# First two batches of a sliding-window attention: bias and mask added by TensorE, 13 output buffers, a new written-out order

## The chip, the cores and the metric

The kernel runs on one core of one Trainium2 chip. The metric is the device time of one execution in microseconds (us); lower is better.

## The reference

```python
# q, k, v: (8 batches, 8 heads, 576 rows, 64)
scores = q @ k.T / 8                                   # per batch and head
rel = pos[:, None] - pos[None, :]
scores = where((rel >= 0) & (rel < 128), scores - slope[h] * abs(rel), -1e9)
x = concat_heads(softmax(scores) @ v)                  # (8, 576, 512); slope[h] = 2 ** -(h + 1)
W = (x @ w_q) @ (x @ w_k).T / 8                        # (576, 576) per batch
out = relu(W @ x) @ w_out                              # (8, 576, 512), float32
```

## The kernel before

Everything is written as named steps. A step has an engine, the steps that it depends on, and, on TensorE, a place in PSUM. PSUM is four pairs (0 to 3) of two banks of 512 float columns. The text ORDER lists all steps in program order as `name:engine`, with P for TensorE (and its pair and bank), A for ScalarE (ACT), D for VectorE (DVE), G for GpSimd (POOL), S for SyncE (SP). Each engine takes its steps strictly in that order; semaphores follow from the dependencies and from the reuse of buffers. So the sequence of the work is fixed by hand, and no scheduler moves anything.

A name is a kind, a batch and a part. The key blocks of a batch are 0 to 3 of 128 rows and 4 of 64; the heads of a unit are u = 0 (heads 0 to 3) or 1 (heads 4 to 7).

- **LF, Lq, Lk, Lt, Lv**: loads. LF are the six float loads of the first blocks, by SP and ACT. The others are issued by POOL (lines 378, 385, 391) and cast to float16; Lt holds the last 64 rows of q and k of two batches, in two DMAs. There are 109 POOL loads. Lw and Lwo (lines 442, 450) fetch the weights on SP's queue.
- **TF, TJ, TQ, TT** and their evictions **EF, EJ, ETQ, ETT**: transposes of q and k on TensorE through an identity matrix (line 251), and copies out of PSUM (lines 255 on ACT, 257 on DVE).
- **QK b.g.u** (line 571): scores of key block g against up to 256 query rows, for four heads, in one pair; 64-row weights, two heads side by side. **EXP** (line 591, ACT) takes the exponential of the whole pair, 1024 columns, into a float16 tile pt. **MUL** (line 598, DVE) multiplies pt by the tile bias (biasl for the last block), which holds exp(-slope * rel) inside the window and 0 outside.
- **PV b.q** (line 622): the product with v, with a column of ones for the sums. **RC** (line 652) and **X** (line 638), both on DVE, divide by the sums and write x. **XT, XTT** with **EXT, EXTT** transpose x.
- Two batches form a group. **WK, WT, WQ, G, MX, RM** work out relu(W @ x) without forming W: projections, the product G of projected keys and x, its product MX with the projected queries, and the eviction RM with the relu. EWK, EWT, EWQ and EG are the evictions between. CWQ and CW cast the weights.
- **OUT** (line 858), **EO** (eviction to a float buffer osb, line 868) and **DO** (store, lines 875 and 878, SP's queue) give the output. The osb buffers are a ring: each tile takes the place of the one allocated OSB tiles before it, and waits until that one has been stored. Float loads and weights use the same ring.
- **GT** makes the next store wait for a QK step, so that stores stay behind loads.
- **WM.i**: products of a zero tile with itself, 256 columns each (line 303), in stretches where TensorE would stand idle; WARM lists how many each stretch has. Their results are not used.
- Set-up steps on DVE: warm, wmc, ones, zeros, biasl, pads, idh (identity in float16); on POOL iota, ident, mask; on ACT bias. The mask tile wm holds rel inside the window and 1e9 outside.

In batches 0 and 1 each QK unit is followed by its own EXP and MUL, as in all others:

```python
s = add("QK", b, f"{g}.{u}", w, pe(0.225), need, em, banks=2, mode=1)
x = add("EXP", b, f"{g}.{u}", w + 0.6, {"ACT": (0.92, 1.02)}, [s, *oldp], ex, frees=[s])
mul[b, g, u] = add("MUL", b, f"{g}.{u}", w + 1.6, DVE(0.68),
                   [x, mkb if g < 3 else mkbl], ml)
```

Of the kernel before, what the change touches and what calls it, by code (L numbers as in the profile page):

```python
# [12 lines left out]
ALU = mybir.AluOpType  # L13
# [20 lines left out]
OSB = 15  # L34
# [11 lines left out]
WARM = (13, 2, 5, 7, 5, 10, 2, 4, 4, 2, 1, 1, 2, 3, 4, 5, 1, 1, 2, 10, 1, 2, 2)  # L46

ORDER = """
warm:D LF0.0.1.1:A LF0.1.0.0:S iota:G WM.0:P01 ident:G wmc:D LF0.0.0.1:S LF0.0.1.0:A ones:D
mask:G LF0.0.0.0:S LF0.1.0.1:S Lq0.2:G bias:A Lk0.1:G zeros:D TF0.1.0:P00 Lt0:G WM.1:P10  # L50
TF0.0.1:P01 EF0.1.0:A biasl:D TF0.0.0:P10 TF0.1.1:P00 WM.2:P20 Lk0.3:G EF0.0.0:A QK0.0.0:P1
EF0.1.1:D Lq0.3:G WM.3:P20 EF0.0.1:D EXP0.0.0:A idh:D Lk0.2:G QK0.0.1:P0 TJ0.2.0:P20 EXP0.0.1:A
TJ0.1.1:P21 EJ0.2.0:D Lk1.3:G WM.4:P30 EJ0.1.1:D MUL0.0.0:D QK0.1.1:P0 Lq1.3:G QK0.1.0:P1
EXP0.1.1:A WM.5:P30 Lq1.2:G EXP0.1.0:A MUL0.1.1:D TT0:P00 Lk1.2:G WM.6:P30 ETT0:D ETT1:A
TJ0.3.1:P01 Lk1.1:G MUL0.1.0:D WM.7:P30 EJ0.3.1:A MUL0.0.1:D TJ0.3.0:P00 Lq1.1:G WM.8:P30
EJ0.3.0:A TJ0.2.1:P01 Lk1.0:G QK0.3.0:P1 EJ0.2.1:D WM.9:P30 EXP0.3.0:A QK0.2.1:P0 Lq1.0:G
WM.10:P30 QK0.3.1:P2 WM.11:P30 EXP0.2.1:A TQ1.3:P10 Lk2.3:G WM.12:P11 ETQ1.3:D EXP0.3.1:A
QK0.2.0:P3 WM.13:P11 Lv0.0:G MUL0.2.1:D TQ1.2:P00 EXP0.2.0:A Lv0.1:G QK1.3.0:P1 ETQ1.2:D
WM.14:P20 EXP1.3.0:A MUL0.3.1:D Lv0.2:G QK1.2.0:P0 TQ1.1:P30 MUL0.2.0:D EXP1.2.0:A Lk2.2:G
QK1.2.1:P1 ETQ1.1:D WM.15:P20 EXP1.2.1:A Lv0.3:G MUL1.2.0:D QK1.1.1:P0 TQ1.0:P30 MUL1.3.0:D  # L60
EXP1.1.1:A Lq2.2:G QK1.1.0:P1 ETQ1.0:D WM.16:P31 QK1.3.1:P2 EXP1.1.0:A WM.17:P31 Lq2.3:G
MUL0.3.0:D PV0.0:P0 QK1.0.0:P3 MUL1.1.1:D EXP1.3.1:A Lv1.0:G MUL1.2.1:D QK1.0.1:P1 EXP1.0.0:A
Lv1.1:G MUL1.1.0:D PV0.1:P2 RC0.0:D EXP1.0.1:A Lv1.2:G X0.0:D PV0.2:P3 RC0.1:D Lk2.0:G X0.1:D
PV0.3:P0 WM.18:P11 RC0.2:D X0.2:D Lv1.3:G TQ2.2:P10 XT0.0:P11 MUL1.3.1:D ETQ2.2:A Lq2.0:G
TQ2.3:P20 MUL1.0.1:D WM.19:P21 ETQ2.3:A Lq2.1:G MUL1.0.0:D RC0.3:D EXT0.0:A PV1.1:P3 X0.3:D
Lk2.1:G QK2.2.0:P2 pads:D PV1.2:P0 RC1.1:D Lv0.4:G EXP2.2.0:A X1.1:D XT0.1:P10 Lv1.4:G wz:D
RC1.2:D QK2.2.1:P3 Lw:S EXT0.1:A X1.2:D PV1.0:P2 Lk3.1:G WM.20:P11 Lwo.2:S RC1.0:D PV1.3:P0
EXP2.2.1:A X1.0:D Lwo.0:S Lq3.1:G WM.21:P11 Lwo.1:S RC1.3:D XT1.0:P10 Lwo.3:S X1.3:D Lt1:G
TQ2.0:P11 EXT1.0:A XT1.1:P00 ETQ2.0:D WM.22:P20 TQ2.1:P01 EXT1.1:D Lq3.0:G PV0.4:P1 ETQ2.1:D
PV1.4:P2 RC0.4:D Lk3.0:G X0.4:D QK2.1.1:P0 QK2.0.0:P3 EXP2.1.1:A Lk3.2:G RC1.4:D QK2.0.1:P1  # L70
X1.4:D Lq3.2:G CWQ:A MUL2.2.1:D QK2.1.0:P0 EXP2.0.0:A XTT0:P20 WK0:P21 Lq4.1:G EXTT0:D
MUL2.1.1:D EXP2.0.1:A Lk3.3:G WT0:P20 EWK0:D WQ0:P30 EWT0:A MUL2.0.0:D Lv2.1:G EXP2.1.0:A G0:P31
EWQ0:D CW.2:A CW.0:D TQ3.1:P10 EG0:A Lq3.3:G CW.1:A ETQ3.1:D MX0.0:P0 MX0.2:P2 RM1.0:A TT2:P11
RM0.2:D RM0.0:A MX0.3:P3 Lt2:G RM1.2:D RM1.3:A MX0.1:P0 ETT2:D RM0.3:A TQ3.0:P10 CW.3:D RM1.1:A
RM0.1:D QK2.3.1:P2 Lv2.0:G OUT1.1:P30 EXP2.3.1:A ETQ3.0:D Lv3.0:G TQ3.2:P31 EO1.1:A MUL2.3.1:D
QK3.0.1:P0 QK2.3.0:P2 Lv2.2:G ETQ3.2:D DO1.1:S EXP3.0.1:A OUT0.3:P10 ETT3:D Lq4.0:G MUL2.0.1:D
EXP2.3.0:A QK3.0.0:P3 QK3.1.1:P0 MUL2.1.0:D Lk4.0:G GT3.0:S OUT1.3:P11 EO0.3:A MUL2.3.0:D
EXP3.1.1:A Lv2.3:G TQ3.3:P20 MUL2.2.0:D OUT1.0:P21 EXP3.0.0:A ETQ3.3:D Lv3.1:G OUT0.1:P10
MUL3.0.1:D EO1.0:A MUL3.0.0:D EO1.3:A QK3.1.0:P0 QK3.3.0:P3 Lk4.1:G MUL3.1.1:D EXP3.1.0:A
QK3.3.1:P2 GT3.1:S GT3.3:S OUT0.2:P11 EO0.1:D Lv3.4:G EXP3.3.0:A MUL3.1.0:D PV2.1:P0 Lv3.2:G  # L80
OUT1.2:P10 EXP3.3.1:A RC2.1:D MUL3.3.0:D Lv3.3:G PV2.2:P3 X2.1:D EO1.2:A QK3.2.1:P2 EO0.2:A
Lv2.4:G RC2.2:D PV2.0:P0 DO1.2:S X2.2:D EXP3.2.1:A OUT0.0:P10 DO0.3:S Lk4.2:G RC2.0:D X2.0:D
TT4:P11 EO0.0:A Lk4.3:G MUL3.3.1:D MX0.4:P3 QK3.2.0:P2 ETT5:A RMT0:D PV3.1:P0 Lq4.3:G GT3.2:S
EXP3.2.0:A XT2.0:P10 MUL3.2.1:D PV2.3:P3 Lq4.2:G RC3.1:D EXT2.0:A MUL3.2.0:D TQ4.0:P20
OUT1.4:P21 RC2.3:D Lq5.3:G X3.1:D ETT4:A ETQ4.0:A X2.3:D PV3.0:P1 TQ4.1:P00 RC3.0:D PV3.2:P3
EO1.4:A X3.0:D Lq5.1:G ETQ4.1:A XT2.1:P01 RC3.2:D X3.2:D XT3.0:P10 Lq5.2:G PV3.3:P2 EXT2.1:A
EXT3.0:D PV3.4:P3 Lq5.0:G RC3.3:D QK4.0.0:P1 X3.3:D PV2.4:P0 Lk5.1:G EXP4.0.0:A GT4.0:S DO1.0:S
RC3.4:D XT3.1:P20 DO1.3:S RC2.4:D Lk5.2:G X2.4:D TQ4.3:P21 EXT3.1:A QK4.0.1:P1 X3.4:D Lk5.3:G
TQ4.2:P00 EXP4.0.1:A WK2:P01 ETQ4.2:D Lk5.0:G ETQ4.3:A XTT2:P20 QK4.1.1:P1 Lk6.3:G EXTT2:D
WQ2:P30 EXP4.1.1:A EWK2:D Lv4.1:G MUL4.0.0:D WT2:P31 EWQ2:D QK4.2.1:P2 EWT2:A QK4.1.0:P0  # L90
EXP4.2.1:A MUL4.1.1:D G2:P10 Lv4.2:G GT4.1:S MUL4.0.1:D EXP4.1.0:A Lk6.2:G QK4.2.0:P3 EG2:D
TQ5.1:P11 EXP4.2.0:A GT4.2:S DO1.4:S Lv4.0:G MX2.0:P0 ETQ5.1:D MX2.2:P2 DO0.1:S RM2.0:A MX2.1:P3
RM3.2:D Lk6.0:G RM3.0:A TQ5.2:P10 RM2.2:D TQ5.3:P11 RM2.1:A Lv4.3:G MUL4.1.0:D RM3.1:A MX2.3:P0
QK4.3.1:P2 RM3.3:A Lq6.0:G ETQ5.3:D TQ5.0:P30 EXP4.3.1:A OUT3.0:P31 ETQ5.2:D Lv5.2:G MUL4.2.0:D
RM2.3:A QK5.3.0:P1 QK5.2.0:P2 ETQ5.0:D EXP5.3.0:A GT5.3:S OUT2.3:P00 GT5.2:S EO3.0:D Lk6.1:G
EXP5.2.0:A OUT3.1:P01 MUL4.3.1:D DO3.0:S MUL4.2.1:D Lv5.1:G EO2.3:A QK5.0.1:P1 QK4.3.0:P3
MUL5.3.0:D EXP5.0.1:A QK5.0.0:P2 Lv4.4:G GT4.3:S OUT2.0:P00 EO3.1:D GT5.0:S EXP4.3.0:A
MUL5.0.1:D Lq6.2:G PV4.2:P1 OUT3.3:P01 EXP5.0.0:A RC4.2:D Lq6.1:G X4.2:D PV4.0:P3 EO2.0:A
MUL4.3.0:D QK5.1.0:P1 QK5.1.1:P2 EO3.3:A RC4.0:D GT5.1:S OUT2.1:P00 Lv5.0:G X4.0:D EXP5.1.1:A
DO3.3:S MUL5.2.0:D TQ6.0:P01 Lq6.3:G EXP5.1.0:A MUL5.1.1:D PV4.1:P3 OUT2.2:P20 Lv5.3:G RC4.1:D  # L100
ETQ6.0:A X4.1:D PV4.3:P1 Lv5.4:G MUL5.1.0:D EO2.2:A QK5.2.1:P3 RC4.3:D Lq7.1:G QK5.3.1:P2
EXP5.2.1:A X4.3:D OUT3.2:P01 MUL5.0.0:D Lk7.0:G EXP5.3.1:A PV4.4:P1 MUL5.2.1:D TQ6.2:P30 Lk7.1:G
RC4.4:D EO3.2:A MUL5.3.1:D XT4.1:P31 ETQ6.2:A PV5.2:P2 X4.4:D Lq7.0:G TQ6.1:P01 EO2.1:A EXT4.1:D
Lt3:G MX2.4:P1 XT4.0:P30 RMT2:A DO2.1:S RC5.2:D TQ6.3:P00 X5.2:D DO2.2:S ETQ6.1:A PV5.1:P1
DO3.2:S ETQ6.3:D DO2.0:S PV5.0:P2 EXT4.0:A Lv6.1:G OUT3.4:P31 RC5.1:D RC5.0:D X5.1:D Lk7.2:G
X5.0:D QK6.0.1:P0 EO3.4:A PV5.3:P1 EXP6.0.1:A Lq7.2:G XT5.0:P20 RC5.3:D X5.3:D PV5.4:P3 EXT5.0:A
Lv6.0:G QK6.1.1:P0 RC5.4:D QK6.2.0:P1 X5.4:D EXP6.1.1:A XT5.1:P21 Lq7.3:G TQ7.1:P20 EXT5.1:D
EXP6.2.0:A Lk7.3:G QK6.2.1:P3 QK6.0.0:P0 MUL6.0.1:D WK4:P21 GT6.0:S EXP6.0.0:A ETQ7.1:D Lv6.3:G
XTT4:P10 MUL6.2.0:D TQ7.0:P11 EXP6.2.1:A QK6.1.0:P0 ETQ7.0:D WQ4:P20 EWK4:A GT6.1:S EXTT4:D
EXP6.1.0:A MUL6.1.1:D WT4:P21 Lv6.2:G MUL6.2.1:D EWQ4:A QK7.0.1:P3 TT6:P10 MUL6.1.0:D EWT4:A  # L110
Lv7.1:G QK7.0.0:P0 EXP7.0.1:A G4:P11 MUL6.0.0:D GT7.0:S DO3.4:S Lv7.0:G ETT6:D EXP7.0.0:A
DO3.1:S QK6.3.1:P2 DO0.2:S EG4:D Lv7.4:G TQ7.2:P30 GT6.2:S EXP6.3.1:A DO0.0:S ETT7:D Lv7.2:G
MX4.2:P0 ETQ7.2:D MX4.3:P1 RM4.2:A MX4.0:P2 RM4.3:D Lv7.3:G RM5.3:A PV6.1:P3 RM5.0:D RM4.0:A
MX4.1:P1 RM5.2:A MUL7.0.0:D Lv6.4:G TQ7.3:P20 RM4.1:A RC6.1:D QK6.3.0:P0 ETQ7.3:D RM5.1:A
OUT4.1:P21 EXP6.3.0:A X6.1:D QK7.2.1:P1 EO4.1:D QK7.3.1:P3 EXP7.2.1:A QK7.2.0:P0 MUL6.3.1:D
OUT5.0:P20 DO4.1:S GT7.2:S GT6.3:S DO2.3:S MUL6.3.0:D EXP7.2.0:A PV6.2:P1 MUL7.0.1:D OUT4.0:P21
EXP7.3.1:A RC6.2:D X6.2:D QK7.1.1:P0 EO5.0:A QK7.3.0:P3 MUL7.3.1:D QK7.1.0:P1 EXP7.1.1:A
OUT5.1:P20 MUL7.2.0:D EXP7.1.0:A MUL7.2.1:D OUT4.2:P00 MUL7.1.1:D EXP7.3.0:A PV6.3:P1 MUL7.1.0:D
OUT4.3:P01 RC6.3:D EO4.0:A X6.3:D EO5.1:A PV7.1:P3 DO4.0:S MUL7.3.0:D EO4.2:A DO5.0:S PV6.0:P1
PV7.2:P2 GT7.1:S EO4.3:A RC6.0:D DO4.2:S RC7.1:D X6.0:D XT6.1:P00 DO5.1:S OUT5.3:P01 DO4.3:S  # L120
RC7.2:D EXT6.1:A X7.1:D GT7.3:S X7.2:D PV7.0:P1 EO5.3:A PV7.3:P3 RC7.0:D XT6.0:P00 X7.0:D
DO5.3:S PV6.4:P2 EXT6.0:A RC7.3:D X7.3:D XT7.0:P01 PV7.4:P1 RC6.4:D EXT7.0:A X6.4:D XT7.1:P30
# [48 lines left out]
def kernel(  # L171
# [54 lines left out]
    def two(bank):  # L226
        return pairs[bank[0]]
# [725 lines left out]
```

## Time and profile before

| | |
|---|---|
| time of three runs | 142.67 us median (142.62 to 142.86) |
| the profiled execution | 142.51 us, its span on the core 140.4 us |
| busy, share of the span | TensorE 93%, ACT 84%, DVE 83%, POOL 68% |
| largest groups | EXP 64 x 1045 ns (ACT), MUL 48 + 16 x about 0.68 us (DVE) |
| DMA | 25.60 MB at a mean of 182 GB/s |

Busy times are those of the profiler; on TensorE products overlap, so a step's cost is read from one start to the next. "PEld" is the loading of weights, beside the products. A row of the timeline gives the start, the length of the merged group, engine, line, operation, output and input, and the count; brackets hold the idle time before it and what ended that.

### The profile page before, as it was taken

The numbers are of one execution on the slowest core, as the hardware profiler recorded it, in microseconds if no ns is written. First come the engines' busy times: TensorE is split into PE (matmuls) and PEld (weight loads), VectorE is DVE, ScalarE is ACT, GpSimd is POOL, SyncE is SP. The second block draws the span as 40 slices with busy tenths as digits, with TensorE's granted clock in tenths as the row PEclk, the third lists the DMA queues.
The fourth block names the chain that finished last, engine by engine and source line by source line (L and its number), as shares of the span: only waits on it lengthen the run. The fifth ranks groups of instructions, "written<-read, shape, count | busy, mean of one in ns | idle before, by whom it ended". The sixth has DMA issues, their size and how long they took to land.

```text
span 140.4 us, 4614 instructions
## 1 busy us (share of the span) xinstructions
PE 131.1 (93%) x1909; PEld 87.7 (62%) x1909; DVE 117.0 (83%) x270; ACT 117.8 (84%) x168; POOL 95.6 (68%) x118
## 2 busy tenths in 40 slices
PE   6999998999898999999999999999899999999970
PEld 5867655868664556788646566978446568753430
DVE  5866399998998999998899999989979999759330
ACT  4868899697599999998899999999989997748340
POOL 7999999999939998999969688996297000000000
PEclk9999999999999999999999999999999999999997
DMA  4999999999999999999999999999999979205593
GB/s 101 199 151 155 150 151 155 150 152 165 258 225 158 159 195 155 185 212 157 237 161 183 212 197 191 161 216 259 163 170 247 211 169 374 79 0 149 161 389 130
DMA packets 119477, 25.60 MB, mean 182 GB/s; under 512 B 114208, under 2 KB 114464, under 8 KB 119456
## 3 DMA queue, kind: packets, MB, share of 16 engines
q0 software_dynamic: 109264, 13.77, 154.7%
q1 hardware_dynamic: 9136, 11.28, 24.2%
q10 hardware_dynamic: 1056, 0.26, 0.8%
q8 instruction: 15, 0.25, 0.6%
q14 instruction: 6, 0.05, 0.1%
HBM read 29.62 MB, written 9.44 MB: 278 GB/s over the span
## 4 chain that ended last, share of the span: by engine, by line
PE 60%; ACT 15%; DMA 7%; DVE 6%; issue 5%; POOL 3%; ACTq 0%
PE pair L248 49%; PE pair L251 11%; ACT pt L591 10%; DMA natt<-in_k_dram 7%; POOL nat L378 2%; ACT rm L785 2%; DVE qkT L257 2%; DVE pt L598 1%; DVE x L638 1%; DVE osb L257 1%; ACT wout_sb L255 1%; ACT xT L255 1%; DVE inv L652 1%; POOL natt L385 1%; ACT wkt L255 0%
## 5 line engine op out<-in xcount | busy, mean ns | idle before, releaser
L591 ACT ACTIVATE pt<-pair 128x1024 f16<-128x1024 f32 x64 | 62.4, 1045 | 5.1 <-PE pair L248 5.0
L391 POOL DMA_DIRECT2D vt<-in_v_dram x40 | 34.7, 896 | 7.9 <-DMA natt<-in_q_dram 4.5
L598 DVE TENSOR_TENSOR pt<-pt,bias 128x1024 f16<-128x1024 f16 x48 | 31.6, 685 | 1.1 <-ACT pt L591 0.9
L248 PE MATMUL pair<-wout_sb,rm 128*128 128x512 f16 (+1 forms) x132 | 31.4, 373 | 0.0
L378 POOL DMA_DIRECT2D nat<-in_k_dram x31 | 28.8, 945 | 1.5 <-issue 0.5
L378 POOL DMA_DIRECT2D nat<-in_q_dram x30 | 28.1, 968 | 1.7 <-DMA vt<-in_v_dram 0.9
L248 PEld LDWEIGHTS <-pt 128*128 128x128 f16 x576 | 20.8, 97 | 5.8 <-issue 2.5
L248 PE MATMUL pair<-vt,pt 128*128 128x65 f16 x576 | 23.1, 193 | 0.9 <-ACT pt L591 0.8
L248 PE MATMUL pair<-qkT 64*128 64x256 f16 (+2 forms) x320 | 22.4, 250 | 0.8 <-ACT pt L591 0.3
L638 DVE TENSOR_TENSOR x<-pair,inv 128x512 f16<-128x512 f32 x32 | 21.7, 686 | 0.8
L257 DVE COPY qkT<-pair 128x1024 f16<-128x1024 f16 (+1 forms) x28 | 16.8, 611 | 5.3 <-PE pair L251 3.2
L255 ACT COPY osb<-pair 128x512 f32<-128x512 f32 (+1 forms) x28 | 15.9, 609 | 3.8 <-PE pair L248 3.8
L251 PE MATMUL pair<-identh,nat 128*128 128x128 f16 x244 | 18.8, 219 | 0.2
L248 PEld LDWEIGHTS <-rm 128*128 128x128 f16 x132 | 11.4, 97 | 12.0 <-issue 1.3
L251 PEld LDWEIGHTS <-nat 128*128 128x128 f16 x244 | 14.7, 98 | 3.8 <-issue 2.3
L248 PEld LDWEIGHTS <-qkT 64*128 64x128 f16 x320 | 10.9, 94 | 9.2 <-issue 4.0
L248 PE MATMUL pair<-warm 128*128 128x256 f16 x89 | 15.2, 299 | 1.1 <-DVE warm L298 1.1
L255 ACT COPY xT<-pair 128x1024 f16<-128x1024 f16 x12 | 12.1, 1023 | 1.7 <-PE pair L251 1.7
L255 ACT COPY qkT<-pair 128x1024 f16<-128x1024 f16 (+1 forms) x13 | 10.9, 866 | 1.7 <-PE pair L251 1.2
L785 ACT ACTIVATE rm<-pair 128x512 f16<-128x512 f32 x21 | 10.9, 623 | 0.0
L598 DVE TENSOR_TENSOR pt<-pt,biasl 128x1024 f16<-128x1024 f16 x16 | 10.8, 679 | 0.1
L248 PEld LDWEIGHTS <-warm 128*128 128x128 f16 x89 | 8.4, 106 | 4.0 <-issue 1.3
(69 smaller groups left out, 136.9 us busy)
## 6 DMA issues: line engine op xcount, KB each, us to landing
out_dram<-osb SPq DMA_DIRECT2D x31, 256.0 KB, 5.3
vt<-in_v_dram POOLq DMA_DIRECT2D x32, 128.0 KB, 6.9
nat<-in_k_dram POOLq DMA_DIRECT2D x31, 128.0 KB, 6.9
nat<-in_q_dram POOLq DMA_DIRECT2D x30, 128.0 KB, 6.9
out_dram<-osb SPq DMA_DIRECT2D x10, 128.0 KB, 2.5
osb<-in_moe_w_out_dram SPq DMA_DIRECT2D x4, 256.0 KB, 6.5
osb<-in_q_dram SPq DMA_DIRECT2D x4, 128.0 KB, 3.3
natt<-in_q_dram POOLq DMA_DIRECT2D x4, 128.0 KB, 8.1
```

The source lines that it names most:

```text
L248: hold(nc.tensor.matmul(*a, **k))
L251: hold(nc.tensor.transpose(*a))
L255: hold(nc.scalar.copy(out_ap, in_ap))
L257: hold(nc.vector.tensor_copy(out=out_ap, in_=in_ap))
L378: return lambda: nc.gpsimd.dma_start(out=natv(b, j, n), in_=(q, k)[j][b, :, P * n:P * n + P, :].transpose([1, 0, 2]))
L385: nc.gpsimd.dma_start(out=natt_s[pr % 2][:, j].rearrange("p e h d -> p (e h) d"), in_=(q, k)[j][2 * pr:2 * pr + 2, :, 512:576, :].rearrang ...
L391: return lambda: nc.gpsimd.dma_start(out=vtv(b, t)[:n, :, 0:D], in_=v[b, :, P * t:P * t + n, :].transpose([1, 0, 2]))
L591: nc.scalar.activation(out=pt[:, 0:1024], in_=two(s.bank).rearrange("p e c -> p (e c)"), func=AF.Exp, scale=SCALE)
L598: ENG2[o.eng].tensor_tensor(out=pt[:, 0:1024], in0=pt[:, 0:1024], in1=bt, op=ALU.mult)
L638: nc.vector.tensor_tensor(out=x[r].rearrange("p (g h d) -> p g h d", g=2, h=4), in0=sums(p)[r, :, :, 0:64], in1=box["inv"][r].unsqueeze(3) ...
L652: nc.vector.reciprocal(out=box["inv"][r], in_=sums(p)[r, :, :, 64])
L785: hold(nc.scalar.activation(out=out_ap, in_=in_ap, func=AF.Relu, scale=WSCALE))
```

## The change

For the units of key blocks 0 to 2 of batches 0 and 1 (twelve of them), TensorE first writes the logarithm of bias and mask into the pair (step **BI**: two products of the identity with a tile blog, 512 columns each), and QK adds the scores to it. EXP follows as before, and MUL is left out. Two tiles blog are made from the mask by eight VectorE operations of 256 columns. The ring of output buffers shrinks from 15 to 13, and the whole order is a new one; WARM has 17 stretches instead of 23, again 89 products in all. Many evictions change between ACT and DVE with the new order.

```diff
-OSB = 15
+OSB = 13
-WARM = (13, 2, 5, 7, 5, 10, 2, 4, 4, 2, 1, 1, 2, 3, 4, 5, 1, 1, 2, 10, 1, 2, 2)
+PEB = {(b, g) for b in (0, 1) for g in range(3)}
+WARM = (13, 3, 3, 8, 12, 2, 1, 8, 4, 11, 4, 3, 5, 5, 2, 2, 3)
...
+    blog = [cpool.tile([P, 2, 2, 256], F16, name=f"blog{u}") for u in range(2)]
...
+    def mk_blog(o, u):
+        for a in range(2):
+            for e in range(2):
+                s = 2.0 ** (2 - (2 * (2 * u + a) + e))
+                nc.vector.tensor_scalar(out=blog[u][:, e, a, :], in0=wm, scalar1=6.0e4 / s,
+                                        scalar2=-s, op0=ALU.min, op1=ALU.mult)
+    mkg = [add("blog", "", u, -19, DVE(1.3), [mask], lambda o, u=u: mk_blog(o, u)) for u in range(2)]
...
-                                         t[r, 0, hp, q0:q0 + wd], start=True, stop=True)
+                                         t[r, 0, hp, q0:q0 + wd], start=not added,
+                                         stop=a == 1 if added else True)
...
+        added = (b, g) in PEB
+        def eb(o):
+            for e in range(2):
+                mm(two(o.bank)[:, e, :], identh, blog[u][:, e].rearrange("p a c -> p (a c)"),
+                   start=True, stop=False)
+        if added:
+            own = add("BI", b, f"{g}.{u}", w - 0.5, pe(0.43), [mkg[u], idh], eb, banks=2)
+            s = add("QK", b, f"{g}.{u}", w, pe(0.225), [own, *need], em, mode=1)
+        else:
+            own = s = add("QK", b, f"{g}.{u}", w, pe(0.225), need, em, banks=2, mode=1)
...
+        if added:
+            mul[b, g, u] = x
+            return
```

TensorE's steps up to the first mix, before and after (pair and bank left out):

```
before: WM.0 TF0.1.0 WM.1 TF0.0.1 TF0.0.0 TF0.1.1 WM.2 QK0.0.0 WM.3 QK0.0.1 TJ0.2.0 TJ0.1.1 WM.4 QK0.1.1 QK0.1.0
WM.5 TT0 WM.6 TJ0.3.1 WM.7 TJ0.3.0 WM.8 TJ0.2.1 QK0.3.0 WM.9 QK0.2.1 WM.10 QK0.3.1 WM.11 TQ1.3 WM.12 QK0.2.0 WM.13
TQ1.2 QK1.3.0 WM.14 QK1.2.0 TQ1.1 QK1.2.1 WM.15 QK1.1.1 TQ1.0 QK1.1.0 WM.16 QK1.3.1 WM.17 PV0.0 QK1.0.0 QK1.0.1
PV0.1 PV0.2 PV0.3 WM.18 TQ2.2 XT0.0 TQ2.3 WM.19 PV1.1 QK2.2.0 PV1.2 XT0.1 QK2.2.1 PV1.0 WM.20 PV1.3 WM.21 XT1.0
TQ2.0 XT1.1 WM.22 TQ2.1 PV0.4 PV1.4 QK2.1.1 QK2.0.0 QK2.0.1 QK2.1.0 XTT0 WK0 WT0 WQ0 G0 TQ3.1 MX0.0 MX0.2 TT2 MX0.3

after: WM.0 TF0.0.0 WM.1 TF0.1.0 TF0.0.1 WM.2 TF0.1.1 BI0.0.0 BI0.0.1 QK0.0.0 QK0.0.1 TJ0.1.1 TJ0.2.0 WM.3 BI0.1.0
BI0.1.1 QK0.1.0 QK0.1.1 TT0 TJ0.3.0 WM.4 TQ1.3 WM.5 TJ0.2.1 WM.6 BI0.2.1 QK1.3.1 BI0.2.0 QK0.2.1 QK0.2.0 QK1.3.0
TQ1.2 WM.7 BI1.2.1 TJ0.3.1 QK1.2.1 WM.8 QK0.3.1 BI1.2.0 QK0.3.0 QK1.2.0 TQ1.1 WM.9 PV0.1 BI1.1.0 BI1.1.1 QK1.1.0
QK1.1.1 PV0.0 PV0.2 WM.10 PV0.3 WM.11 TQ1.0 XT0.0 TQ2.1 XT0.1 WM.12 PV1.3 BI1.0.0 BI1.0.1 QK1.0.0 QK1.0.1 WM.13
PV1.2 WM.14 TQ2.2 WM.15 XT1.1 WM.16 TQ2.3 QK2.1.1 PV1.0 PV1.1 QK2.2.1 QK2.2.0 PV1.4 XT1.0 TQ2.0 PV0.4 QK2.1.0
QK2.0.1 QK2.0.0 XTT0 WK0 WT0 WQ0 G0 TT2 MX0.0 MX0.2 MX0.1 MX0.3
```

Between them on ACT after the last EXP of batch 1: before `ETQ2.2 ETQ2.3 EXT0.0 EXP2.2.0 EXT0.1 EXP2.2.1 EXT1.0 EXP2.1.1 CWQ EXP2.0.0 EXP2.0.1 EWT0 EXP2.1.0 CW.2 EG0`, after `EXP2.1.1 EXP2.2.1 EXP2.2.0 EXT1.0 CWQ EXP2.0.1 CW.2 EXP2.0.0 EWK0 EXP2.1.0 EG0`. The late stores on SP: before `GT6.2 DO0.0 DO4.1 GT7.2 GT6.3 DO2.3 DO4.0 DO5.0`, after `GT6.3 DO2.2 GT7.2 DO3.2 DO2.1 DO4.1 DO3.3 DO3.0 GT7.3 DO5.0`. By the new allocation EO4.3 takes the buffer of DO3.0; before it took that of DO1.4.

## The prediction

> **What bounds the kernel now.** I read the page first, then the busy times of three stretches, the zero products alone, TensorE's waits, and last the timeline around the joints.
>
> ```profile
> PE 131.1 (93%) x1909; PEld 87.7 (62%) x1909; DVE 117.0 (83%) x270; ACT 117.8 (84%) x168; POOL 95.6 (68%) x118
> ...
> PE 60%; ACT 15%; DMA 7%; DVE 6%; issue 5%; POOL 3%; ACTq 0%
> ```
>
> TensorE (PE) is busiest and carries 60% of the chain that ended last. The next answer cuts the span at 38.3 us, where the first projection WK0 starts, and at 101.5 us, where the last wait of TensorE for a load ends. The second fence has the zero products alone.
>
> ```profile
> 0.00:38.30 38.30, 35.24 (x486) 26.02 (x487) 30.59 (x104) 29.90 (x40) 37.52 (x51) 1.00 2.05 161
> 38.30:101.50 63.20, 61.61 (x992) 41.43 (x990) 59.62 (x114) 61.66 (x90) 52.37 (x61) 1.00 2.19 191
> 101.50:136.10 34.60, 34.24 (x436) 20.26 (x436) 26.48 (x54) 26.23 (x40) 5.74 (x7) 1.00 1.01 191
> ```
>
> ```profile
> 0.00:38.30 38.30, 15.21 (x89) 8.36 (x89) 0.17 (x1) 1.00 2.05 161
> 38.30:101.50 63.20, 0.00 (x0) 0.00 (x0) 0.00 (x0) 1.00 2.19 191
> ```
>
> Columns: stretch, length, then busy time and count of PE, weight loads, DVE, ACT, POOL (second fence: PE, weight loads, DVE); the 1.00 is the granted clock. In the first stretch PE looks full, but 89 of its products are zero products. Behind 38.3 us all three engines are full, and PE barely waits:
>
> ```profile
> PE pair L251 <- DMA natt<-in_k_dram: 0.7, 1, 0.7
> PE pair L248 <- ACT pt L591: 0.3, 1, 0.3
> PE pair L248 <- ACT gs L255: 0.3, 1, 0.3
> PE pair L248 <- ACT rm L785: 0.3, 1, 0.3
> ```
>
> So behind 38.3 us the time is PE's own work; ahead of it PE has room only as far as it waits or multiplies zeros. The question is whether the added products displace zeros and waits, or come on top.
>
> **Pitches** (start to start on PE):
>
> ```profile
> 1.06 2.96 PE L248 MATMUL pair<-warm 128*128 128x256 f16 x13 [1.06 <-DVE warm L298]
> 9.72 0.61 PE L248 MATMUL pair<-qkT 64*128 64x256 f16 x8
> 27.70 1.26 PE L248 MATMUL pair<-warm 128*128 128x256 f16 x10
> 37.73 0.39 PE L248 MATMUL pair<-qkT 64*128 64x256 f16 x4 [0.32 <-ACT pt L591]
> 128.91 7.09 PE L248 MATMUL pair<-wout_sb,rm 128*128 128x512 f16 x36
> ```
>
> The first 13 zero products run until 3.81, where the next step starts: 0.212 each. Later ones: ten take 1.26 and a lone one shows 0.28, so (1.26-0.28)/9, 0.107 rounded with the other rows. A product of 512 columns: 36, of which 8 are half as long, take 7.09, less some 0.2 of tail over 32: 0.215. A QK step of 4: 0.61-0.39, 0.225. Where PE goes from a 64-row step (QK, TT, MX) to a 128-row one or back, 0.10 more: QK1.2.0 starts at 18.77, the next step at 19.10. Others, from the same starts: TJ 0.22, TT 0.47, TQ 0.445, PV 0.48 (first 0.26), XT 0.45, XTT 0.22, WK 0.93, WT 0.36, WQ 0.865, G 1.18, MX 0.215 (tail 0.12), OUT 0.86.
>
> **PE up to WK0, before.** 15 cold and 74 warm zero products 3.18+7.92=11.10; TF 2.08, 5 TJ 1.10, TT 0.47, 8 TQ 3.56, 22 QK 4.95, 10 PV 4.36, 4 XT 1.80, XTT 0.22, together 18.54; 36 changes of rows 3.60; start 1.06. Sum 34.30. WK0 starts at 38.29: 3.99 of waits.
>
> **The same, after.** The new order has exactly the same steps ahead of WK0, plus 12 BI. It still has 89 zero products: 16 cold 3.39, 73 warm 7.81. BI: 24 products of 512 columns at 0.215, 5.16 (nearest rows: OUT 0.215; bounds 0.107, the 256-column pitch, and 0.38, the mean length of a lone 512-column row: 2.6 to 9.1; I take 0.215, the same width, rows and type back to back). Changes of rows: 24, since BI and QK stand in pairs: 2.40. Sum 1.06+11.20+18.54+5.16+2.40=38.36. **With no wait at all PE reaches WK0 no earlier than now.** So the added products don't displace the zeros; they displace only waits, of which there were 3.99.
>
> The Trainium skill's page "TensorE: Matmul & The Clock Gate" (Back-to-back issue gap) gives about 131 ns for a sustained 512-column product with its weight load; by that BI would be 3.1 and the sum 2.0 less. The trace disagrees: 0.215 in the row above, where each product has its weight load too.
>
> Waits of the new order, walked along the queues with the rows' lengths (EXP 0.97, MUL and X 0.69, RC 0.20, ETQ 1.0 on ACT or 0.69 on DVE; 0.2 from PE's last product to its reader):
> - near 9 to 11: TJ0.1.1 waits for its load (landed 8.18), the eight zeros of WM.3 for EXP0.0.0 (they write its pair), QK0.1.0 for EJ0.1.1, which stands behind two EXPs: 0.5. Everything on PE queues behind, so EXP0.1.1 starts near 11.2 against 10.16.
> - near 14: QK1.3.1 for ETQ1.3, on DVE behind ones, zeros, biasl: 0.1.
> - near 25 to 28: PV0.3, TQ1.0 and TQ2.1 take pairs that X0.0, X0.2 and X0.3 must clear: 0.5.
> - near 36 to 40: XT1.0 for X1.1, QK2.1.0 for ETQ2.0 behind X1.4, XTT0 for X0.4: 0.8.
>
> Together 1.9: WK0 near 40.3, **+2.0**. Bounds: 0.1 (no wait) and +4.1 (as many waits as before).
>
> **What DVE and ACT lose.** Twelve MUL at 0.685, 8.2, leave DVE; eight blog steps come. No row has this operation; 256 columns from float cost 0.21 (copy) to 0.35 (smallest eviction): 1.7 to 2.8 in all, from 2.6 us on. EF0.0.0 stands behind them, until about 6.0; QK0.0.0 on PE is at 7.5 by the sum above, so that is hidden by 1.5 us; without cover it is 0.7 at most. The freed 5.4 us buys nothing while PE sets the pace; ETQ and EXT steps move from ACT to DVE ahead of WK0, so ACT has 2.7 us less there, also off the path. POOL has the same 33 loads up to the last of these batches, now Lv0.4; the last one landed at 35.38 before (Lv1.4), and I take the same.
>
> **Behind WK0** both orders hold the same 183 steps and 64 changes of rows: QK 9.45, TQ 8.90, TT 1.41, PV 13.08, XT and XTT 6.06, projections with G 13.34, MX 3.92, OUT 30.96, changes 6.40: 93.5. Before took 38.3 to 135.4, 97.1: 3.6 of waits. What changes: EWK0 goes to ACT behind EXP2.0.1, CW.2 and EXP2.0.0, and G0 waits for it (0.4); MX0.0 waits for EG0 (0.4), MX0.3 for the RM of its pair (0.35), QK2.3.0 for RM0.1 (0.4): 1.6 against 0.9 before, **+0.7**. TT6 waited 0.85 for Lt3; a PE that comes 2.7 later finds it there, with some small ones **-1.0**.
>
> Sum: 2.0+0.7-1.0=+1.7. The profiled execution took 142.51 (span 140.4 and 2.1 around it): 144.2. The median shown is 142.67, 0.16 above it, less than this sum can tell, so I leave 144.2.
>
> **Rivals.**
> *Loads set the first two batches, not PE: faster.* Place: Lv0.4 lands at 35.4, then PV0.4 0.5, hand-over 0.25, RC and X 0.9, XTT0 with its start 0.3: WK0 at 37.4, since one X follows instead of two.
>
> ```profile
> 36.27 0.68 DVE L638 TENSOR_TENSOR xtl<-pair,inv 64x512 f16<-64x512 f32 x1
> 36.99 0.21 DVE L652 RECIPROCAL inv<-pair 64x8 f32<-64x8 f32 x1
> 37.23 0.69 DVE L638 TENSOR_TENSOR xtl<-pair,inv 64x512 f16<-64x512 f32 x1
> ```
>
> These two X_.4 in a row now end at 37.92 and release XTT0. With ACT ahead, no new wait at the mix: -0.9, 141.6. It decides if PE's work ahead of WK0 is 1.0 less than 37.3, say a change of rows costing 0.06. Against it: the sum. Chance 0.13.
>
> *Later waits swallow the delay:* if 2.7 of the 3.6 behind WK0 are waits for loads, 142.5. Against: only 0.7 to 0.9 shows a DMA as releaser. 0.10.
>
> *The new holes fit as badly as the old:* waits 4.0 again, +4.1+0.7-1.0: 146.3. For: waits of this size stand in this trace. 0.15.
>
> *The ring of 13:* EO4.3 now takes the buffer that DO3.0 must have stored; DO3.0 is sixth in a row of stores released by QK6.3.0 and QK7.2.0, and stores in such rows land 6 to 9 us after the first is issued (issues from 90.19, fourth landed 99.40). It decides once DO3.0 lands after OUT4.3 ends; ACT then stops, and XT6.1 needs that bank: about 1.0 on top, 145.2. 0.12.
>
> *BI at its lower bound:* the weights of the next product load beside the one that streams, and 24 products take 2.6 instead of 5.2: 141.6. The 0.215 of the OUT rows, loaded in the same way, speaks against it: 0.02. The Trainium skill's 131 ns above points to this side.
>
> **How the numbers follow.** Forecast 0.48. What this measurement can tell from no change is about 0.2%, 142.4 to 143.0. Faster: the two rivals at 141.6 and the lower ends of the others, 0.17; same 0.07, mostly swallowed delays; slower 0.76. The range goes from 142.0, between the first two rivals, to 146.4, just past the badly fitting holes; about 0.1 is left out on each side.
>
> **What would show it.** WK0's first product near 40.3 (under 38.3 breaks the sum); BI products 0.215 apart; zero products still 0.107; wait before G0 released by ACT wk; no DMA wait at TT6; 95 to 96 us from WK0 to the last product. I am wrong if PE reaches WK0 by 38.5 or loses under 2 us behind it.

## Result: 0.9% slower

The changed kernel takes 143.84 us in the median of 16 runs (143.54 to 144.44), the kernel before 142.62 us on the same chips (16 runs, 142.05 to 143.93). The ratio is 1.0086, 95% interval 1.0067 to 1.0104. The forecast was 144.2 us, slower. The profiled execution of after took 143.94 us, its span 142.2 us (before 142.51 and 140.4).

The page of after, busy times and the engines' shares of the chain that ended last:

```profile
PE 135.0 (95%) x1933; PEld 91.1 (64%) x1933; DVE 113.8 (80%) x269; ACT 116.3 (82%) x165; POOL 95.6 (67%) x118
...
PE 75%; ACT 14%; DVE 5%; issue 3%; DVEq 0%; ACTq 0%
```

TensorE has 3.9 us more of busy time, VectorE 3.2 us less, and TensorE's share of the chain is 75% where it was 60%; the 7% of DMA are gone. The engine that was relieved was not the one that set the end. The busy times cut at WK0 (40.84 us now, 38.29 before), then the zero products alone; columns as in the prediction:

```profile
0.00:40.84 40.84, 38.88 (x509) 28.74 (x510) 27.77 (x99) 27.89 (x37) 39.95 (x53) 1.00 2.02 161
40.84:138.00 97.16, 96.16 (x1428) 62.37 (x1424) 85.60 (x171) 88.39 (x129) 55.68 (x65) 1.00 1.74 188
```

```profile
0.00:40.84 40.84, 14.23 (x89) 8.78 (x89) 0.17 (x1) 1.00 2.02 161
```

The first row grew by 2.55 us. The 89 zero products are all still there, and of the stretch's 40.84 us TensorE is busy for 38.88. The step rows of TensorE in this stretch (start, length, and in brackets the idle time before):

```profile
9.40 1.03 PE L250 MATMUL pair<-warm 128*128 128x256 f16 x8 [0.34 <-ACT pt L613]
10.27 1.03 PE L250 MATMUL pair<-blog,identh 128*128 128x512 f16 x4
11.22 0.61 PE L250 MATMUL pair<-qkT 64*128 64x256 f16 x8
...
12.46 1.47 PE L250 MATMUL pair<-warm 128*128 128x256 f16 x12
13.87 0.61 PE L253 MATMUL pair<-identh,nat 128*128 128x128 f16 x8
```

Eight zero products wait for an exponential, because they write a pair that it still reads (line 613 is EXP), and everything behind them in TensorE's queue waits as well. At 12.46 twelve more hold the queue for 1.41 us. Four BI products run from 10.27 to 11.22: 0.95, which is four at 0.215 and a change of rows.

TensorE's waits over the whole span (total, times, longest):

```profile
PE pair L250 <- DVE warm L300: 1.1, 1, 1.1
PE pair L250 <- DVE rm L812: 0.4, 1, 0.4
PE pair L250 <- ACT pt L613: 0.3, 1, 0.3
PE pair L253 <- DVE xtl L663: 0.2, 1, 0.2
```

No DMA is left in the list, where before Lt3 alone stood for 0.7 us. From WK0 to the start of the last step of products there are 96.5 us and to the end of the last product 97.1, both 0.6 fewer than before.

### The profile page after: what moved, and what is told of

It reads as the page before. It is cut to its first block, busy times and chain, and to the rows that moved or that the text cites. A ratio compares the mean times of both kernels' runs of the same rounds, so it can differ in the third digit from the quotient of the medians.

```text
span 142.2 us, 4683 instructions
## 1 busy us (share of the span) xinstructions
PE 135.0 (95%) x1933; PEld 91.1 (64%) x1933; DVE 113.8 (80%) x269; ACT 116.3 (82%) x165; POOL 95.6 (67%) x118
## 4 chain that ended last, share of the span: by engine, by line
PE 75%; ACT 14%; DVE 5%; issue 3%; DVEq 0%; ACTq 0%
PE pair L250 60%; PE pair L253 16%; ACT pt L613 10%; ACT rm L810 2%; DVE x L663 1%; DVE qkT L259 1%; DVE osb L259 1%; ACT wqT L257 1%; ACT xT L257 1%; DVE inv L677 1%; DVE xtl L663 0%; ACT gs L257 0%; ACT wkt L257 0%; DVE xTt L259 0%; DVE warm L300 0%
## 5 line engine op out<-in xcount | busy, mean ns | idle before, releaser
L388 POOL DMA_DIRECT2D nat<-in_k_dram x31 | 29.6, 962 | 1.1 <-PE pair L253 1.1
L388 POOL DMA_DIRECT2D nat<-in_q_dram x30 | 29.0, 973 | 1.0 <-DMA nat<-in_k_dram 0.7
L620 DVE TENSOR_TENSOR pt<-pt,bias 128x1024 f16<-128x1024 f16 x36 | 23.6, 685 | 0.6 <-ACT pt L613 0.5
L250 PE MATMUL pair<-qkT 64*128 64x256 f16 (+2 forms) x320 | 21.0, 250 | 0.0
L257 ACT COPY osb<-pair 128x512 f32<-128x512 f32 x26 | 14.7, 622 | 3.0 <-PE pair L250 3.0
L250 PE MATMUL pair<-warm 128*128 128x256 f16 x89 | 14.2, 299 | 1.5 <-DVE warm L300 1.1
L259 DVE COPY osb<-pair 128x512 f32<-128x512 f32 (+1 forms) x11 | 7.1, 641 | 6.8 <-PE pair L250 6.1
L257 ACT COPY xT<-pair 128x1024 f16<-128x1024 f16 x11 | 10.9, 1013 | 1.9 <-PE pair L253 1.9
```

Of the source, the lines that this page charges most:

```text
L250: hold(nc.tensor.matmul(*a, **k))
L257: hold(nc.scalar.copy(out_ap, in_ap))
L259: hold(nc.vector.tensor_copy(out=out_ap, in_=in_ap))
L388: return lambda: nc.gpsimd.dma_start(out=natv(b, j, n), in_=(q, k)[j][b, :, P * n:P * n + P, :].transpose([1, 0, 2]))
L620: ENG2[o.eng].tensor_tensor(out=pt[:, 0:1024], in0=pt[:, 0:1024], in1=bt, op=ALU.mult)
```

## Experiments

Three theories. **Theory 1**, the prediction's: TensorE's own queue sets WK0, BI comes on top of zero products that are rigid in it, and WK0 sets the end. **Theory 2**: the zero products are needed to keep the clock, and cost nothing beside that. **Theory 3**: the new order itself, with its moved evictions, or the smaller ring, costs the time. "WK0" below is the start of its first product in the profiled execution; every ratio is against the kernel before on the same chip.

WK0 comes from a single execution, and these don't start alike. Up to the first BI the variants of after that keep BI have the same steps, and yet the first BI starts between 6.42 and 7.38 us (the last section says why). The rows are, in this order, from after, BI products twice, no zero products, zeros cut to the holes, the last five groups removed, and two evictions moved:

```profile
6.93 1.03 PE L250 MATMUL pair<-blog,identh 128*128 128x512 f16 x4
6.42 1.89 PE L250 MATMUL pair<-blog,identh 128*128 128x512 f16 x8
6.49 1.03 PE L250 MATMUL pair<-blog,identh 128*128 128x512 f16 x4
7.38 1.03 PE L250 MATMUL pair<-blog,identh 128*128 128x512 f16 x4
7.04 1.03 PE L250 MATMUL pair<-blog,identh 128*128 128x512 f16 x4
6.76 1.03 PE L247 MATMUL pair<-blog,identh 128*128 128x512 f16 x4
```

So for these runs the time from the first BI to WK0 is given too; in after it is 40.84 - 6.93 = 33.91 us. That WK0 sets the end is shown by all runs together: in the ten with WK0 at 38.77 us or later the last product ends 97.1 to 97.3 us behind WK0; only before (97.7) and the run without zeros in its order (97.6) wait for a load there.

**No zero products behind the first 19, in the order of after.**

```diff
-WARM = (13, 3, 3, 8, 12, 2, 1, 8, 4, 11, 4, 3, 5, 5, 2, 2, 3)
+WARM = (13, 3, 3, 0, 0, 0, 0, 0, 0, 0, 0, 0, 0, 0, 0, 0, 0)
```

> The changed kernel without the 70 zero products behind the first 19 (no real work is left out). Theory 1 (TensorE's queue sets WK0, and the zero products in it are rigid): 70 at 0.107 us, 7.5 us, leave the queue ahead of WK0, which then waits for loads and evictions instead: the last value load of these batches landed at 35.2 us, its eviction chain and XTT0 take about 2 us more, so WK0 at 37.2 to 38.5 us instead of 40.84, time 140.3 to 141.8 us. Theory 2 (the zero products are needed to keep the clock): the granted clock falls below 1.00 in some stretch ahead of 45 us, products there are twice as far apart, and the time is 145 us or more. Theory 3 (the new order of evictions costs the time, the added products do not): under 0.5 us gained, 143.3 to 143.8 us.

Measured: 142.32 us, ratio 0.9973 (0.9952 to 0.9993), WK0 at 38.80. The gain over after is 1.5 us in the median and 2.04 at WK0; from the first BI to WK0 it is 1.60 (32.31 instead of 33.91), and 0.44 is an earlier start. That comes from 7.5 us of products: the rest turned into waits.

```profile
10.35 0.61 PE L250 MATMUL pair<-qkT 64*128 64x256 f16 x8 [0.81 <-ACT qkT L257]
...
12.99 0.72 PE L253 MATMUL pair<-identh,nat 128*128 128x128 f16 x10 [1.24 <-ACT pt L613]
```

TensorE now waits for ScalarE, and ScalarE and VectorE carry 19% and 9% of the chain. So three limits lie close together: TensorE's queue at 40.84, the evictions at 38.8, and the last load of these batches at 34.9, with some 2 us of steps behind it by the expectation. Theory 1 had the sign, but missed both its ranges, WK0 by 0.3 and the time by 0.5 us. Theory 3's 143.3 us does not fit the median. Theory 2 shows in one run of the twelve: it had a mean granted clock of 0.980 and took 144.12 us, the others 0.993 or more and at most 142.44.

**No zero products behind the first 20, in the order of before.**

```diff
-WARM = (13, 2, 5, 7, 5, 10, 2, 4, 4, 2, 1, 1, 2, 3, 4, 5, 1, 1, 2, 10, 1, 2, 2)
+WARM = (13, 2, 5, 0, 0, 0, 0, 0, 0, 0, 0, 0, 0, 0, 0, 0, 0, 0, 0, 0, 0, 0, 0)
```

> The kernel before without the 69 zero products behind the first 20 (no real work is left out). Theory 1: its WK0, at 38.29 us, already stood on the chain of the last value load (35.38 us), so it comes at most 0.6 us earlier: 141.9 to 142.6 us. Theory 2 (zeros needed for the clock): granted clock below 1.00 ahead of 45 us and 145 us or more. If the time falls by over 1 us, the zero products held up the kernel before as well.

Measured: 142.59 us, ratio 1.0017 (0.9992 to 1.0042), WK0 at 38.50. The time lies in theory 1's range, though WK0 came 0.2 later and not earlier. In the kernel before the zero products cost nothing; without them TensorE waits about as long as it multiplied zeros. But the clock does fall, in all twelve runs: their mean granted clock is 0.956 to 0.985, against 0.992 or more in the 23 runs of before on the same chip. The windows of the profiled execution show it (the last three columns are the granted clock, the DMA share and GB/s):

```profile
7.00:10.50 3.50, 1.90 (x25) 1.13 (x25) 2.22 (x6) 2.63 (x3) 3.50 (x5) 1.00 2.25 143
10.50:14.00 3.50, 2.53 (x28) 2.01 (x28) 2.32 (x4) 2.75 (x5) 3.50 (x5) 0.57 2.38 152
14.00:17.50 3.50, 3.06 (x35) 2.16 (x34) 0.88 (x2) 2.80 (x4) 3.50 (x5) 0.50 2.36 156
17.50:21.00 3.50, 2.51 (x36) 1.56 (x36) 3.50 (x7) 3.50 (x5) 3.50 (x5) 0.95 2.42 151
```

```profile
9.37 0.61 PE L248 MATMUL pair<-qkT 64*128 64x256 f16 x8 [0.76 <-ACT pt L591]
10.88 0.94 PE L251 MATMUL pair<-identh,natt 64*128 64x64 f16 x16 [0.89 <-ACT pt L591]
```

The three rows of a lower clock make about 6.9 us at half speed (2 x 0.43, 0.50 and 0.05 of 3.5 us). In them TT0's sixteen products take 0.87 to the next step instead of 0.56. Theory 2 is half right: zeros hold the clock here, but its fall cost this kernel no measurable time, and the 145 us did not come. That the slower products took the place of waits would explain it; no run here shows it by itself. The Trainium skill's page "TensorE: Matmul & The Clock Gate" (HAM oscillation — how this bites in real kernels) names idle gaps of more than some 3.4 us as what loses the clock. The trace disagrees: the longest waits ahead of the fall, after the first product, were 0.76 and 0.89, in a stretch where TensorE was busy for 1.90 us of 3.50.

**MUL instead of BI, in the order of after.** Zero products and 13 buffers stay.

```diff
-PEB = {(b, g) for b in (0, 1) for g in range(3)}
+PEB = set()
-... blog.0:D ... blog.1:D ... BI0.0.0:P1 ... BI0.0.1:P3 ... QK0.0.0:P QK0.0.1:P ...
+... QK0.0.0:P1 QK0.0.1:P3 ... MUL0.0.0:D ... MUL0.0.1:D ...
```

> The changed kernel's order, zero products and 13 buffers, but the bias is multiplied on VectorE again in the first two batches: no BI, no blog, twelve MUL placed some 8 words behind their EXP. Theory 1: 5.16 us of products leave TensorE's queue, WK0 is then set by waits and loads: 37.5 to 39.0 us instead of 40.84, time 141.0 to 142.5 us. Theory 3 (the new order or the smaller ring costs the time): 143.4 us or more, WK0 within 0.4 us of 40.84.

Measured: 143.91 us, ratio 1.013 (1.0083 to 1.0177; six runs, two of them at 145.5), WK0 at 40.38. Theory 1's 37.5 to 39.0 is missed: 5.16 us left TensorE's queue and brought 0.46. The windows from 8 to 28 us, first this kernel, then after (busy PE, PEld, DVE, ACT, POOL), show why:

```profile
8.00:16.00 8.00, 5.93 (x84) 4.53 (x83) 7.40 (x38) 4.45 (x6) 8.00 (x10) 1.00 2.36 151
16.00:28.00 12.00, 10.67 (x172) 8.37 (x167) 11.24 (x22) 9.43 (x11) 12.00 (x15) 1.00 2.39 153
```

```profile
8.00:16.00 8.00, 7.66 (x95) 5.49 (x91) 5.37 (x37) 4.53 (x6) 8.00 (x10) 1.00 2.25 145
16.00:28.00 12.00, 11.95 (x175) 8.58 (x174) 7.44 (x15) 9.31 (x10) 12.00 (x15) 1.00 2.38 151
```

VectorE is full in the first pair of rows (7.40 of 8.00, 11.24 of 12.00) and carries 18% of the chain; TensorE has room. In the second pair it is the other way round. By the prediction's pitches this order needs 32.80 us up to WK0 without waits (38.36 less BI and four changes of rows), so 7.6 us are waits. The time is theory 3's (143.4 or more), WK0 just outside its 0.4 us. By the rows the cause is VectorE's full queue, and in after that queue has room: the new order gave VectorE evictions in place of the MULs, and here it has both.

**The same with VectorE relieved:** six evictions back on ScalarE, the MUL where VectorE had room.

```diff
-EJ0.3.0:D ETT1:D EJ0.3.1:D EXT0.0:D ETQ2.2:D ETQ2.3:D   (each at its place in ORDER)
+EJ0.3.0:A ETT1:A EJ0.3.1:A EXT0.0:A ETQ2.2:A ETQ2.3:A
```

> As the earlier run with MUL in the changed kernel's order (no BI, no blog), but VectorE is relieved: ETT1, EJ0.3.0, EJ0.3.1, EXT0.0, ETQ2.2 and ETQ2.3 go back to ScalarE as in the kernel before, and the twelve MUL stand where VectorE had room. Theory 1 (the products cost the time; the run before this one only put VectorE in their place): WK0 at 38.0 to 39.5 us, time 141.4 to 142.9 us. Theory 3 (the order of loads, scores and evictions itself costs it): WK0 at 40.2 us or later, 143.3 us or more.

Measured: 145.39 us, ratio 1.0191 (1.0166 to 1.0217), WK0 at 41.63. A miss for theory 1 again, within theory 3's numbers. TensorE waited 3.4 us for X on VectorE ahead of WK0, in whose queue X0.0 to X0.3 now stood behind MULs, and 1.7 for loads. So relieving VectorE of evictions did not bring the order with MUL back. My placing is part of this number, so it does not tell what the best order with MUL could do; the kernel before, at 38.29, is a better answer to that.

**BI instead of MUL, in the order of before.** Zero products as before; 14 buffers.

```diff
-QK0.0.0:P1 ... MUL0.0.0:D ...
+BI0.0.0:P1 QK0.0.0:P ...          (all twelve, straight ahead of one QK or two)
+blog.0:D idh:D blog.1:D           (behind bias:A; ones, zeros, biasl behind them)
```

> The kernel before, its order and its zero products, but in the first two batches TensorE adds the logarithm (each BI straight ahead of its QK step or of a run of them) and the twelve MUL are gone; 14 buffers, since 15 do not fit beside the new tables. Theory 1 (TensorE's queue: added products come on top of zeros and displace only waits): no-wait sum 34.3+5.2 and some changes of rows, WK0 at 40.0 to 42.5 us instead of 38.29, time 144.2 to 146.7 us. Theory 3 (the added products are harmless, the new order costs the time): WK0 under 38.9 us, time 142.2 to 143.1 us.

Measured: 146.84 us, ratio 1.0294 (1.0267 to 1.0321), WK0 at 42.97, 4.68 later than before. That is 5.16 us of products almost undiminished: theory 1, with WK0 0.5 above its range and the time 0.1. The changes of rows are 36 as before, so the sum without waits is 34.30 + 5.16 = 39.46, and the waits are 3.5 us instead of 4.0.

The four orders together, by WK0: before 38.29, BI added 42.97, new order without BI 40.38, both 40.84. Each part alone makes it later, by 4.68 and by 2.09, and together by 2.55. The added products cost 4.7 us in the old order. The new order is the worse one with MUL, as theory 3 has it, and with BI it wins 2.1 of the 4.7 back. In the prediction's terms that is 1.1 of the sum without waits (39.46 to 38.36, the changes of rows that fall from 36 to 24) and 1.0 of waits (3.5 to 2.5). So theory 1 and theory 3 each hold for one part alone, and the two parts save each other 4.68 + 2.09 - 2.55 = 4.22 us at WK0. The MULs of the order without BI are placed by me, so 2.09 is an upper bound, and each of the four is a single execution.

**BI products twice** in the order of after (24 more products of 512 columns that change nothing).

```diff
-for e in range(2):                                        # stop=False
+for e, last in ((0, True), (1, True), (0, False), (1, False)):   # stop=last
```

> The changed kernel with every BI product issued twice into the same bank (24 more products of 512 columns that add nothing to the result). Theory 1: 24 at 0.215 us, 5.2 us more in TensorE's queue, less what they take over of the 2.5 us of waits ahead of WK0: WK0 at 43.5 to 46.0 us, time 146.5 to 149.0 us. Theory 3 (the added products lie beside other waits): under 1 us more, up to 144.8 us. If a product costs only 0.107 us: at most 2.6 us more, up to 146.4 us.

Measured: 148.99 us, ratio 1.0471 (1.0432 to 1.0509), WK0 at 45.52, both in theory 1's ranges: 4.68 later than after. But this execution started its first BI 0.51 earlier. From the first BI to WK0 it took 39.10 us, 5.19 more than after, and 24 at 0.215 are 5.16: the added products cost their full length, and no wait took any of it over. It settles the price of a product, and it shows that TensorE's queue has no slack left in after. A cost of 0.107 (at most 2.6 us in all) is ruled out.

**13 output buffers, in the kernel before.**

```diff
-OSB = 15
+OSB = 13
```

> The kernel before with 13 output buffers instead of 15, nothing else. Theory 1 (the ring plays no part): 142.2 to 143.0 us, no output copy waits for a store. Theory of the ring: the late output copies of batches 4 and 5 wait for stores, 143.1 us or more.

Measured: 142.20 us, ratio 0.9974 (0.9953 to 0.9996); no engine waits for a store. The ring costs nothing, and it even gains 0.4 us in the median, at the lower end of theory 1's range. The gain is not in the span, which is 140.4 us in the median of both kernels, but in the time around it: 2.16 us in the median of the 23 runs of before (2.09 to 2.29), 1.81 here (1.73 to 1.90). Why fewer buffers shorten it is open. In its profiled execution WK0 started at 38.80, half a microsecond later than before, as the last of the first float loads landed at 6.44 instead of 5.83, and the span was 140.4 us all the same: half a microsecond at WK0 can be absorbed behind it, where before waits 0.7 us for Lt3 and this run does not.

**Without the zeros, two evictions moved,** to see whether the evictions were the next limit.

```diff
 (on top of the run without zero products in the order of after)
-EJ0.2.0:D zeros:D EJ0.1.1:A
+EJ0.1.1:D EJ0.2.0:D zeros:D
-ETQ2.3:D
+ETQ2.3:A
```

> The changed kernel without the 70 zero products behind the first 19, and with two evictions moved: EJ0.1.1 goes back to VectorE ahead of the clearing of the tails (it stood behind two exponentials on ScalarE), ETQ2.3 to ScalarE (it stood in VectorE's last row of evictions before WK0). Theory 1 (without the zeros the eviction chains on ScalarE and VectorE set WK0, 38.80 us in the earlier run): WK0 0.2 to 0.8 us earlier, 38.0 to 38.6 us, time 141.4 to 142.2 us. If TensorE or the loads set it: WK0 at 38.8 us, 142.3 us again.

Measured: 143.58 us (12 runs, 142.01 to 144.84), ratio 1.0055 (1.0023 to 1.0087), WK0 at 38.77, no gain against the run without zeros, and the time missed theory 1's 141.4 to 142.2. From the first BI to WK0 there is a gain, 32.01 instead of 32.31 us, which a start 0.27 later hides. One wait moved on to a load:

```profile
12.49 0.62 PE L250 MATMUL pair<-identh,nat 128*128 128x128 f16 x8 [1.33 <-DMA nat<-in_q_dram]
```

QK0.1.0 started at 9.75 instead of 10.35, but then TQ1.3 waited for Lq1.3, which landed at 12.44; later QK2.2.0 waited for ETQ2.3 on ScalarE. The spread is the second finding: of the twelve runs the seven at a mean granted clock of 0.974 to 0.985 took 143.3 to 144.8 us, the other five, at 0.992 or more, 142.0 to 143.9. Without zeros a small shift decides whether the clock falls. Theory 2 has this much right.

**Zeros cut to the holes.** The run without zeros shows how long each hole is; the new list has 59 products (the text below counts 55), 30 fewer than after, and WM.3 writes a free pair.

```diff
-WARM = (13, 3, 3, 8, 12, 2, 1, 8, 4, 11, 4, 3, 5, 5, 2, 2, 3)
+WARM = (13, 3, 3, 4, 9, 0, 0, 4, 1, 10, 3, 2, 0, 0, 4, 0, 3)
-WM.3:P10
+WM.3:P00
```

> The changed kernel with its zero products cut to the holes that the run without them showed (55 instead of 89, WM.3 with 4 in a free pair instead of 8 in the pair that EXP0.0.0 still reads). Theory 1 (a zero costs only where it overfills its hole): WK0 at 38.8 to 39.4 us instead of 40.84, time 141.9 to 142.7 us. Theory 2 (holes keep the clock): the granted clock stays at 0.99 or more in every run, where the runs without zeros showed some at 0.974 to 0.985 that took 1 to 2 us longer. If the zeros don't count beyond their number: 34 fewer at 0.107 us, 3.6 us, WK0 near 37.2.

Measured: 142.25 us (12 runs, 141.77 to 143.20), ratio 0.9993 (0.9969 to 1.0017). The time is in theory 1's range and the clock was 0.992 or more in all twelve runs. WK0, at 39.70 in the profiled execution, is 0.3 late, but the whole delay lies ahead of the first BI: TensorE's products kept their slow pace of the start longer (TF0.0.1 took 0.85 to the next step, against 0.44 without zeros), and this execution was the slowest of the twelve. From the first BI to WK0 it took 32.32 us, as much as without any zeros (32.31). So the 40 zeros behind the first 19 cost nothing here. With 30 fewer zeros and WM.3 in another pair the changed kernel loses its whole disadvantage; which of the two edits does how much was not run apart. It stands level with the kernel before, not ahead of it, and level with that kernel with 13 buffers too (142.20 us, on another chip).

**Only the last five groups of zeros removed.**

```diff
-WARM = (13, 3, 3, 8, 12, 2, 1, 8, 4, 11, 4, 3, 5, 5, 2, 2, 3)
+WARM = (13, 3, 3, 8, 12, 2, 1, 8, 4, 11, 4, 3, 0, 0, 0, 0, 0)
```

> The changed kernel without its last five groups of zeros (WM.12 to WM.16, 17 products, 1.8 us of queue), which stand between 29 and 35 us. Theory 1: in the run without zeros TensorE gained 0.85 us between XT0.1 and QK2.1.1, so WK0 comes 0.8 to 1.0 us earlier, 39.8 to 40.0 us, time 142.8 to 143.1 us; the clock stays, since the early groups are there. If all 17 lie on the path: 1.8 us earlier. If zeros are not the limit: no change, 143.8 us.

Measured: 142.87 us, ratio 1.0020 (1.0001 to 1.0039), WK0 at 40.10, 0.74 earlier than after, in an execution whose first BI was 0.11 later. From the first BI to WK0 it took 33.06 us, 0.85 less than after, as expected. 17 products are 1.8 us of queue; 0.85 lay on the path, and the rest was in holes.

## Why the prediction was right

- **PE up to WK0, no-wait sum 38.36.** Right. The new order has no room: WK0 came at 40.84, 2.48 us of waits above the sum. The first BI started at 6.93, by the same prices at 6.85.
- **Pitch of BI 0.215.** Right, by the rows above and by doubling it. The 131 ns of the Trainium skill's page "TensorE: Matmul & The Clock Gate" (Back-to-back issue gap), weighed against it in the prediction, do not hold for this stream: two products with their weights take 0.43 to the next step.
- **Waits walked, 1.9.** Mis-sized by 0.6. The places named held: 0.5 at WM.3, 0.35 at PV0.3, 0.7 from XT1.0 to XTT0. The 0.1 near 14 was 0.13 at TQ1.3. What was not walked: 0.31 at XT1.1 (X1.2 ran from 33.19 to 33.88), 0.16 at QK2.2.0, and small ones. WK0 +2.55 instead of +2.0.
- **What DVE and ACT lose.** blog took 2.85 us, just above the 1.7 to 2.8, and was hidden as said: EF0.0.0 ended at 6.05, QK0.0.0 started at 7.89.

```profile
L250 PE MATMUL pair<-blog,identh x24: 378/379/390, 6.9 to 30.9; 128*128 128x512 f16 x24
L365 DVE TENSOR_SCALAR blog<-wm x8: 274/290/658, 2.6 to 4.8; 128x256 f16<-128x256 f32 x8
```

(Minimum, median and maximum in ns, first and last start in us; a product lasts 379 ns and still lets the next one start 215 ns after it. The mean of a blog operation is 2.85 over 8, 0.36. The prediction's 0.21 was the row of a float16 copy; no row of 256 float columns is that short.) "Buys nothing while PE sets the pace" held: ScalarE waited 8.9 us for score products up to 45 us, 3.9 before.
- **Behind WK0, -0.3.** Measured -0.6, but by other parts than forecast. The waits in the mix were expected at 1.6 and came to about 1.05: 0.2 ahead of G0 (released by ACT wk, as said), 0.28 at MX0.0, 0.57 at MX0.3, none at QK2.3.0. They were to cost 0.7 more than before; yet BI in the old order has the same 97.1 us from WK0 to the end of the last product as after, so the new order costs nothing there. TT6's wait for Lt3 went as expected, and the 0.6 is about that wait; the -1.0 of the prediction was too large. The sign "95 to 96 us" was set below the prediction's own 96.8; measured 96.5. Its 93.5 counts the last step whole, while its 97.1 ends at that step's start, so it has the waits 0.4 too low, in both orders alike.

```profile
PEld L250 <- ACT wk L257: 0.5, 1, 0.5
```

- **The sum.** +2.55-0.6 is +1.95 to the last product and +1.8 in the span, against +1.7. The times of the profiled executions differ by 1.4 only, since the time around the span, which the prediction kept at 2.1, fell to 1.7; over the 16 runs of after it is 1.78 in the median. The run with 13 buffers in the old order has 1.81, so the smaller ring goes with it (the second order with MUL, 1.99, is an exception with 13 buffers). The medians differ by 1.2, since the profiled execution of after is slightly above its median (143.94 to 143.84) and that of before below (142.51 to 142.62). So the sign and the mechanism were forecast, but it was luck that the time came so near: 0.55 too little ahead of WK0 met 0.3 too much behind it, 0.15 at the end of the span and 0.4 around it.
- **Rivals.** *Loads:* Lv0.4 landed at 35.17 and was used at 38.84, so it set nothing. *Later waits swallow the delay:* 0.6 of 2.55, less than the 2.7 that it needed. *Holes fit as badly:* in part, 2.5 us of waits instead of 4.0. *The ring of 13:* XT6.1 came without a wait, and in the separate run 13 buffers gained 0.4 us instead of costing. *Lower bound of BI:* refuted.

What the prediction did not see: that the zero products were 1.6 us too many for this order (from the first BI to WK0), until evictions and loads set the pace. It took them as work of the queue, which was right for the time, and did not ask what the kernel would do without them.

## What to carry to other kernels

Work moved to an engine that fills its idle time with dummy products does not displace them: in an in-order queue they cost their full length once the hole is smaller than they are, so size them by the hole that a run without them shows. Before relieving one engine, compare the sum without waits of the engine that takes the work with the time at which the next stage starts now; here that sum alone gave the sign. After the change, find the second limit by removing the first: evictions and loads stood under 2 us behind TensorE, so no more than that could be won. And compare single executions from a point that the start does not move: here the starts differed by up to 1 us, and that hid a gain of 0.3 and made a price of 5.19 look like 4.68.

## What the hardware showed that was not expected

The granted clock fell to 0.50 for about 6.9 us with no single wait between products longer than 0.89 us ahead of it, when TensorE was busy for just over half of a 3.5 us window. In the other order without zeros, waits of 0.81 and 1.24 us left it at 1.00 in the profiled execution. What exactly decides is open.

The first products run at half their later pace, and for how long differs from execution to execution. In after the products of 256 columns still stand 0.213 apart at 4.66, and 0.109 from 6.38 on; without zero products they stand 0.109 apart from 4.29 on, and with the zeros cut to the holes still 0.213 at 6.58. The windows show a granted clock of 1.00 in these stretches all the same. With the landing of the first loads this moves the first BI by up to 1 us in kernels whose steps up to there are the same.
